# The last two block pairs of a down projection taken together, and their stores on two queues

## The chip, the cores and the metric

The kernel runs on one core of a Trainium2 chip. The metric is the device time of one launch in microseconds. A core has five engines, each with an instruction queue of its own: TensorE (PE, matrix products), VectorE (DVE), ScalarE (ACT), GpSimd (POOL) and SyncE (SP, which only issues transfers). SP, ACT and POOL can each issue DMA transfers; semaphores order the engines among each other. The profile is one execution, recorded by the hardware profiler.

## The reference

Two stages. The first is linear attention with decay over 4 batches, 8 heads, 768 positions and 64 dimensions per head; per block of 64 positions it does this:

```python
intra = np.einsum('bhic,bhjc->bhij', qb, kb) * Dmask[None]
intra = np.einsum('bhij,bhjd->bhid', intra, vb)
inter = np.einsum('bhid,bhde->bhie', qb * lam_pow[None], kv_state)
out[:, :, sl] = intra + inter
kv_state = lam_block * kv_state + np.einsum('bhsd,bhse->bhde', kb * rev_pow, vb)
```

Its output, seen as 3072 tokens of 512 values, goes through a feed-forward block with 2048 inner values:

```python
h = x @ w_in                    # 3072 x 512 by 512 x 2048
g = np.maximum(0.01 * h, h)     # leaky ReLU
return (g @ w_out).astype(np.float32)   # 3072 x 2048 by 2048 x 512
```

q, k, v are float32, the two weights arrive as 64-bit floats and are narrowed on the chip.

## The kernel before, in words

**Tiling.** The tokens are cut into six groups of T = 512 tokens. The inner dimension of 2048 is cut into NP = 8 pairs of two blocks of 128 (`p` = 0 to 7). A float32 product is formed from three TensorE products of float32r parts: each operand is split in parts h, l and m, and h by h, l by l and m by m are added into the same PSUM bank. So one block of 128 by 128 weights by 512 tokens costs three matmuls (`product`, L839 to L842).

**Stages.** Attention makes x; `up` (L704) multiplies by w_in, applies the leaky ReLU and stores g in DRAM; the down projection reads g again. It works on three double groups `pr` of 1024 tokens, each with two groups `gi`. For a group the 512 outputs lie in four PSUM banks, one for each 128 outputs (`c` = 0 to 3): banks X and Z for `gi` = 0, banks Y and V for `gi` = 1 (`BANKS`, L795). Banks 0 and 1 of the last group are Y, banks 2 and 3 are V. Some pairs are combined over both groups by Strassen's scheme (`strassen`), the others go through `plain`: for a pair it loads g of the group (512 KB) into a slot of a ring of five (`unit`), ACT makes the part h, DVE the parts l and m, and PE does 2 blocks x 4 banks x 3 parts = 24 matmuls. The work of the last group ends with the pairs 4, 5, 6 and 7 in `plain`.

**Output.** For the last pair of a group, `plain` is called with `last` and takes the banks one by one: six matmuls finish a bank, then DVE turns it over in 32 by 32 blocks into the staging tile `gst` (`turn_out`, L905), and DMAs store it (`store_out`, L912). A bank's 512 tokens are two halves `m` of 256 tokens, which lie in different places of the output, and a store takes one half and a quarter `a` of the 128 rows: eight stores for four banks, of 128 KB each. In the last group of all (`end`), the banks come in the order 2, 3, 0, 1; banks 2 and 3 are stored for themselves (eight stores of 64 KB), then banks 0 and 1; bank 1, the last, is done in two halves of 256 columns. `ENDS` (L915) names the queue of each of these stores: S for SP, A for ACT, P for POOL.

**Order.** Nothing is scheduled by the language: `Plan` takes all operations with a cost in us, what they read and write, and a rank, and lists them by a greedy simulation. At each step, of all operations on all engines it takes the one that can start first, and the lower rank where two can start together (`emit`, L83). Each engine's queue then has that order. `seq` lists the stages, and an operation's rank is its stage's place there, shifted by its own `rank`; the loads of `unit` come LEAD = 8 stages ahead. The semaphore waits follow from which tile regions overlap. These are put in by the framework.

Of the kernel before, what the change touches and what calls it, by code (L numbers as in the profile page):

```python
# [25 lines left out]
S = 4096.0  # L26
# [10 lines left out]
class Plan:  # L37
# [23 lines left out]
    def add(self, eng, us, fn, reads=(), writes=(), rank=0.0):  # L61

        n, deps = len(self.ops), set()
        for k in reads:
            w, r = self.last.setdefault(k, [None, []])
            if w is not None:
                deps.add(w)
            r.append(n)
        for k in writes:
            w, r = self.last.setdefault(k, [None, []])  # L70
            if w is not None:
                deps.add(w)
            deps.update(r)
            self.last[k] = [n, []]
        deps.discard(n)
        ways = {eng: us} if isinstance(eng, str) else dict(zip(eng, us))
        if self.slack:
            self.more[n] = self.slack
        if self.chain is not None:
            self.chains[self.chain].append(n)  # L80
        self.ops.append((ways, fn, deps, (self.rank + rank, n), set(writes)))
# [81 lines left out]
def kernel(  # L163
# [10 lines left out]
    nc = tc.nc  # L174
    P = 128
# [6 lines left out]
    NP = d_ff // (2 * P)  # L182
    NCH = B * NCB
    GC = 4
    NG = NCH // GC
    T = GC * C
# [12 lines left out]
    NS = 4  # L199
    LEAD = 8.0  # L200
# [4 lines left out]
    C4 = P // 4  # L205
# [32 lines left out]
    HT = T // 2  # L238
# [42 lines left out]
    add = plan.add  # L281
# [75 lines left out]
    def run(c):  # L357

        lo = max(DV, c - c % TURN)
        return lo, c - c % TURN + TURN - lo  # L360
# [423 lines left out]
    acc = {"X": flat[:2], "Z": flat[2:], "Y": [b1[0], b2], "V": [b1[1], bank["pt"]]}  # L784
    ACC = {"X": ["X0", "X1"], "Z": ["Z0", "Z1"], "Y": ["b10", "b2"], "V": ["b11", "pt"]}
# [9 lines left out]
    BANKS = [[("X", 0), ("X", 1), ("Z", 0), ("Z", 1)], [("Y", 0), ("Y", 1), ("V", 0), ("V", 1)]]  # L795
# [72 lines left out]
    def plain(pr, p, gi, lead, last=False, banks=None):  # L868

        g = 2 * pr + gi  # L870
        here = plan.rank
        plan.rank -= lead
        d = G[pr][p].rearrange("p (f h t) -> p f h t", f=2, h=2)[:, :, gi, :]
        j = unit(d, [x for x in plan.last if x[0] == "G" and x[1] in (str(2 * pr), str(2 * pr + 1)) and x[2:4] == f"{p}{gi}"], 2)
        plan.rank = here
        reads = [f"r{z}{j}" for z in "hlm"] + [f"w{z}{p}" for z in "hlm"]

        def go(fs, cs, lo=0, n=T):
            for f in fs:
                for c in cs:  # L880
                    d, i = BANKS[gi][c]
                    product(acc[d][i][:, lo:lo + n], j, f * T + lo,
                            lambda z, f=f, c=c: W[p][z][:, f * 2 * NQ + c * P:f * 2 * NQ + (c + 1) * P], first=pr == p == f == 0, n=n)

        if not last:
            add("PE", 0.227 * 24, lambda: go((0, 1), range(4)), reads, [ACC[d][i] for d, i in BANKS[gi]])
            return
        end = pr == NG // 2 - 1 and gi == 1
        for i, c in enumerate(banks):
            d, b = BANKS[gi][c]  # L890
            parts_ = 2 if end and i == 3 else 1
            for half in range(parts_):
                k = ACC[d][b] + (f"half{half}" if parts_ > 1 else "")
                n = T // parts_
                add("PE", 0.227 * 6 * (1.0 if parts_ == 1 else 0.53), lambda c=c, half=half, n=n: go((0, 1), (c,), half * n, n),
                    reads + ([ACC[d][b]] if parts_ > 1 else []), [k])
                turn_out(c, acc[d][b], [ACC[d][b], k], half * n, n)
                if i == 3 or end and i == 1:
                    cs = sorted(banks[:2] if end and i == 1 else banks[2:] if end else banks)
                    for m in ([half] if parts_ > 1 else range(2)):  # L900
                        store_out(pr, gi, m, cs, end)

    otile = gst.rearrange("p x f (b c j) -> p (x f b) c j", c=4, j=C4)

    def turn_out(c, b, keys, lo, n):  # L905
        nonlocal n_o
        n_o += 1
        o = otile[:, lo // C4:(lo + n) // C4, c, :]
        add("DVE", 0.1 + 0.6 * n / T, lambda: nc.vector.transpose(out=o, in_=b[:, lo:lo + n].rearrange("p (b i) -> p b i", i=C4)), keys,
            [f"o{c}{m}" for m in range(lo // HT, (lo + n) // HT)] + (["gs0", "gs1"] if n_o <= 4 else []), rank=-1.5)  # L910

    def store_out(pr, gi, m, cs, last):  # L912
        t0, n, w = (2 * pr + m) * T + gi * HT, HT // C4, len(cs) * C4

        ENDS = {(8, 0): "PSAP", (8, 1): "PSAP", (4, 0): "SAPP", (4, 1): "SASA"}  # L915
        QUEUES = {"S": ("DMA", 0.5, nc.sync), "A": ("ACT", 0.5, nc.scalar), "P": ("POOL", 0.65, nc.gpsimd)}

        def store(a, q):
            c0 = a * P + cs[0] * C4
            q.dma_start(out=out[t0:t0 + HT, c0:c0 + w].rearrange("(b i) j -> i b j", i=C4),  # L920
                        in_=otile[a * C4:(a + 1) * C4, m * n:(m + 1) * n, cs[0]:cs[-1] + 1, :].rearrange("i b c j -> i b (c j)"))

        for a in range(4):
            e, us, q = QUEUES[ENDS[8 if cs[0] > 1 else 4, m][a] if last else "A"]
            add(e, us, lambda a=a, q=q: store(a, q), [f"o{c}{m}" for c in cs], [], rank=-1.5 if last else 6.0)

    def copy_banks(d, s):
        for i in range(2):
# [2 lines left out]
    def add_banks(d, s):  # L931
        for i in range(2):
            y, key = w32[:, i, :], [f"w32{i}"]
            add("ACT", 0.6, lambda i=i, y=y: nc.scalar.copy(y, acc[s][i]), [ACC[s][i]], key, rank=-LEAD)
            add("DVE", 0.72, lambda i=i, y=y: nc.vector.tensor_tensor(acc[d][i], acc[d][i], y, op=ALU.add), key, [ACC[d][i]], rank=-LEAD)

    seq = [("a", 0), ("a", 1), ("a", 2), ("a", 3), ("wi", 1), ("b", 4), ("r", 4), ("up", 0, 1), ("wi", 0), ("r", 5),
# [26 lines left out]
    for pr in range(NG // 2):  # L964
# [3 lines left out]
        def n(p, gi, r=pr):  # L968
            return ("n", r, p, gi) if p < NP - 1 else ("l", r, p, gi, (0, 1, 2, 3) if gi == 0 else (2, 3, 0, 1))
# [6 lines left out]
        else:  # L976
            i = seq.index(("up", NG - 1, NP - 1))
            seq[i:i] = [n(0, 0)]
            seq += [n(0, 1), n(1, 0), n(1, 1), ("ws", 0), n(2, 0), n(2, 1), ("ws", 1), n(3, 0), n(3, 1), ("ws", 2), n(4, 0), n(5, 0), ("ws", 3), n(6, 0), n(7, 0)]
    seq += [n(p, 1) for p in range(NS, NP)]  # L980

    freed = False
    for n, x in enumerate(seq):
        plan.rank = float(n)
        steady = begin <= n and x[0] in ("r", "up", "wo")
        if x[0] in "abr":
            {"a": alone, "b": begun, "r": round_of}[x[0]](x[1])
        elif x[0] == "ls":
            load_subs(DV)
            turn(DV)  # L990
        elif x[0] == "lt":
            load_subs(sum(run(DV)))
        elif x[0] == "wi":
            w_in(x[1])
        elif x[0] == "up":
            up(*x[1:])
        elif x[0] == "wo":
            w_out(*x[1:])
        elif x[0] == "wp":
            if not freed:  # L1000
                add("DVE", 0.0, lambda: None, [], ["psc", "po", "X0", "X1", "Z0", "Z1"])
                freed = True
            w_out_parts(x[1])
        elif x[0] == "ws":
            if x[1] == 0:
                add("DVE", 0.0, free_attention, [], ATT + [f"e{z}{p}" for z in "hlm" for p in range(NS)])
            w_sums(x[1])
        elif x[0] == "fr":
            add("ACT", 0.0, free_raws, [], [f"raw{i}" for i in range(NRAW)] + ["rh4", "rl4", "rm4", "zr"])
        elif x[0] == "s":  # L1010
            strassen(*x[1:], LEAD)
        elif x[0] == "n":
            plain(*x[1:], LEAD)
        elif x[0] == "copy":
            copy_banks(*x[1:])
        elif x[0] == "add":
            add_banks(*x[1:])
        else:
            plain(*x[1:4], LEAD, True, x[4])
    plan.emit()  # L1020
# [30 lines left out]
```

## Time and profile before

| | us |
|---|---|
| median of 3 runs | 604.32 |
| lowest and highest of them | 602.46, 983.98 |
| the profiled execution's own time | 603.61 |
| its span, first to last instruction | 601.8 |
| PE busy | 587.2 (98%) |
| DVE, ACT, POOL busy | 391.1, 291.7, 135.6 |
| mean granted PE clock | 0.996 |

The span starts with the first instruction of the program. PE's busy time is the union of its matmuls as the profiler models them. The stages of the last double group are seen in the timeline by the tile that a matmul writes: `psc` is X, `po` is Z, `b` is Y and the first bank of V, `pt` the second bank of V. The instructions of the store line are shown as queue entries (SPq, ACTq) where SP or ACT issues, and as POOL where GpSimd does; their duration is that of issuing. When the data has arrived is a time of its own, the landing.

### The profile page before, as it was taken

The page shows a single profiled execution, that of the slowest core. Times are in us where ns is not written, and L with a number is a line of the kernel's source. Part 1 is how long each engine was busy: PE and PEld are TensorE (multiplying, and loading weights), DVE is VectorE, ACT ScalarE, POOL GpSimd, SP SyncE. Part 2 cuts the span into 40 slices and gives each one's busy share as a digit, 9 for nine tenths or more (in the row PEclk, how much of TensorE's full clock was granted, in tenths as well). Part 3 has the DMA queues.
Part 4 walks back from the last instruction along what each step waited for, and adds up shares of the span by engine and source line. Part 5 has one row for each costly group of instructions (what it writes and reads, how often), then busy time and mean ns, then how long its engine had stood idle before and what let it go on. Part 6 is the DMA issues. An engine that isn't in the chain of part 4 may idle for free.

```text
span 601.8 us, 13238 instructions
## 1 busy us (share of the span) xinstructions
PE 587.2 (98%) x5340; PEld 486.4 (81%) x5340; DVE 391.1 (65%) x533; ACT 291.7 (48%) x459; POOL 135.6 (23%) x176
## 2 busy tenths in 40 slices
PE   7899999999999999999999999999999999999995
PEld 6677888888788888888788888888888888888884
DVE  5999772534365664464279749975689595788741
ACT  4678974445555555565587754432244223252300
POOL 1654560554647374230000000000000000000002
PEclk9999999999999999999999999999999999999998
DMA  9998864795889999886688635526467456484433
GB/s 212 231 269 237 238 188 121 180 243 145 223 250 249 257 247 256 256 237 229 201 288 305 213 117 198 159 90 192 125 197 224 168 159 191 121 271 148 161 106 70
DMA packets 161357, 119.89 MB, mean 199 GB/s; under 512 B 98736, under 2 KB 137904, under 8 KB 161296
## 3 DMA queue, kind: packets, MB, share of 16 engines
q1 hardware_dynamic: 146160, 109.40, 62.3%
q10 hardware_dynamic: 12384, 5.58, 3.6%
q0 software_dynamic: 2752, 4.07, 2.7%
q8 instruction: 42, 0.69, 0.5%
q14 instruction: 19, 0.16, 0.1%
HBM read 79.17 MB, written 39.85 MB: 198 GB/s over the span
## 4 chain that ended last, share of the span: by engine, by line
PE 86%; DVE 5%; issue 4%; DMA 2%; SPq 2%; POOL 1%; ACT 1%; POOLq 0%; DVEq 0%; ACTq 0%
PE b L716 40%; PE po L841 12%; PE psc L841 11%; PE b L841 11%; PE pt L841 4%; PE po L328 4%; PE psc L328 3%; SPq L389 1%; DVE w L610 1%; DVE w L609 1%; DMA raws<-in_k_dram 1%; DMA xm<-g 1%; PE pt L418 1%; DMA att<-in_k_dram 1%; DVE att L474 1%
## 5 line engine op out<-in xcount | busy, mean ns | idle before, releaser
L716 PE MATMUL b<-xh,wh 128*128 128x512 f32 (+2 forms) x392 | 103.4, 387 | 1.1 <-ACT xh L522 0.8
L716 PE MATMUL b<-xm,wm 128*128 128x512 f32 (+2 forms) x392 | 104.0, 392 | 0.0
L716 PE MATMUL b<-xl,wl 128*128 128x512 f32 (+2 forms) x392 | 103.2, 387 | 0.6 <-DVE wl L621 0.6
L818 ACT ACTIVATE xh<-xm 128x1024 fp32r<-128x1024 f32 x45 | 47.7, 1061 | 93.4 <-DMA xm<-g 42.6
L716 PEld LDWEIGHTS b<-xh,wh 128*128 128x128 f32 x392 | 72.9, 188 | 16.3 <-ACT xh L522 0.9
L716 PEld LDWEIGHTS b<-xl,wl 128*128 128x128 f32 x392 | 72.8, 188 | 15.7 <-DVE wl L621 1.0
L716 PEld LDWEIGHTS b<-xm,wm 128*128 128x128 f32 x392 | 71.5, 188 | 14.9
L734 ACT ACTIVATE b<-b 128x512 f32<-128x512 f32 (+2 forms) x97 | 56.2, 581 | 55.6 <-PE b L716 55.5
L739 ACT ACTIVATE gs<-b 128x512 f32<-128x512 f32 (+2 forms) x97 | 57.2, 592 | 48.7 <-PE b L716 40.1
L920 POOL DMA_DIRECT2D out_dram<-gs x6 | 3.5, 588 | 319.3 <-issue 319.3
L821 DVE SCALAR_TENSOR_TENSOR xl<-xm,xh 128x1024 fp32r<-128x1024 f32 x45 | 54.8, 1218 | 30.0 <-ACT xh L818 29.2
L825 DVE SCALAR_TENSOR_TENSOR xm<-xl,xh 128x1024 fp32r<-128x1024 f32 x48 | 58.7, 1224 | 3.3
L467 DVE TENSOR_TENSOR att<-psc,att 128x512 f32<-128x512 f32 x24 | 16.5, 687 | 47.1 <-PE psc L328 47.1
L477 POOL TENSOR_TENSOR att<-att 128x256 f32<-128x256 f32 x40 | 33.7, 841 | 38.0 <-DVE att L474 37.9
L438 POOL TENSOR_TENSOR att<-att 128x512 f32<-128x512 f32 (+1 forms) x20 | 24.5, 1223 | 71.4 <-PE po L328 50.0
L389 POOL DMA_DIRECT2D att<-in_q_dram x64 | 39.7, 625 | 3.0 <-DVE att L398 1.7
L609 DVE TENSOR_SCALAR w<-w 128x512 int32<-128x512 int32 x32 | 19.3, 604 | 27.5 <-ACT w L603 27.5
L328 PEld LDWEIGHTS po<-att 64*64 64x64 f32 x1472 | 27.1, 134 | 9.5 <-issue 6.5
L610 DVE CUSTOM_DVE_ANT_0 w<-w,lows 128x1024 uint16<-128x1024 uint16 x32 | 29.8, 930 | 7.5 <-ACT lows L607 6.1
L328 PE MATMUL po<-att 64*64 64x64 f32 x1472 | 32.9, 222 | 1.2 <-DVE att L506 0.5
L841 PE MATMUL b<-xl,wl 128*128 128x512 f32 (+1 forms) x86 | 33.0, 384 | 0.0
L841 PE MATMUL b<-xm,wm 128*128 128x512 f32 (+1 forms) x86 | 33.0, 384 | 0.0
(153 smaller groups left out, 1073.8 us busy)
## 6 DMA issues: line engine op xcount, KB each, us to landing
g<-gs SPq DMA_DIRECT2D x31, 512.0 KB, 3.9
xm<-g SPq DMA_DIRECT2D x25, 512.0 KB, 4.5
xm<-b SPq DMA_DIRECT2D x23, 512.0 KB, 3.8
raws<-in_moe_w_in_dram SPq DMA_DIRECT2D x16, 512.0 KB, 5.4
raws<-in_moe_w_out_dram SPq DMA_DIRECT2D x16, 512.0 KB, 4.5
b<-gs SPq DMA_DIRECT2D x16, 512.0 KB, 4.1
att<-in_k_dram SPq DMA_DIRECT2D x48, 128.0 KB, 4.8
att<-in_v_dram SPq DMA_DIRECT2D x24, 256.0 KB, 5.0
```

Of the source, the lines that this page charges most:

```text
L328: nc.tensor.matmul(dst[HALF[cols]], lhsT=lhsT[HALF[rows]], rhs=rhs[HALF[rows]], start=start, stop=True, skip_group_check=True)
L389: (move if nm == "k" else carry)(0.55 if nm == "k" else QSL, lambda o=o, z=z, e=nc.sync if nm == "k" else nc.gpsimd: e.dma_start(out=o.rea ...
L477: add("POOL", 0.7, lambda new=new, j=j: nc.gpsimd.tensor_tensor(state[(j + 1) % 4], new, _bc(lam_c, 2, D), op=ALU.mult), [f"st{j % 4}", "f ...
L609: add("DVE", 0.42, lambda: nc.vector.tensor_scalar(d, d, 3, None, op0=ALU.logical_shift_left), [], [key])
L610: add("DVE", 1.0, lambda: nc.vector.tensor_tensor(d, d, low, op=ALU.add), [kl], [key])
L716: nc.tensor.matmul(dst, lhsT=w[z][:, kk * 2 * P + f * P:kk * 2 * P + (f + 1) * P], rhs=x[z][:, kk, toks], start=start and kk == 0, stop=kk ...
L734: add("ACT", ns, lambda b=b: nc.scalar.activation(out=b, in_=b, func=AF.Copy, bias=0.0, scale=S + 1.0), [], [kb], rank=-1.5)
L739: add("ACT", t, lambda o=o, x=s_: nc.scalar.activation(out=o, in_=x, func=AF.Prelu, bias=0.0, scale=(1.0 + 1.0 / S) / (WS * U), alpha=0.01 ...
L818: nc.scalar.activation(out=ring[j][0], in_=g(), func=AF.Copy, bias=0.0, scale=NEAR)
L821: nc.vector.scalar_tensor_tensor(ring[j][1], g(), 1.0, ring[j][0].bitcast(F32), op0=ALU.mult, op1=ALU.subtract)
L825: nc.vector.scalar_tensor_tensor(m, l.bitcast(F32), -S, h.bitcast(F32), op0=ALU.mult, op1=ALU.add)
L841: nc.tensor.matmul(dst, lhsT=lhs(z), rhs=ring[j][z][:, col:col + n], start=first and z == 0, stop=z == 2, skip_group_check=True)
```

## The change

The pairs 6 and 7 of the last group are no longer two stages but one (`ending`). It does banks 2 and 3 for pair 6, then banks 2 and 3 for pair 7, each turned over as it is done, and stores both; then banks 0 and 1 for pair 6, and for pair 7 first the half `m` = 0 of bank 0 and of bank 1, then the half `m` = 1 of bank 0 and of bank 1, each half turned over by itself, and the half's four stores follow. All sixteen of these stores are issued by SP and ACT in turns. The outputs of the other groups keep their order and their queue. A bank's half is named in the plan by the bank itself, so the second half waits until the first has been turned over.

```diff
+        def some(c, lo=0, n=T):
+            d, b = BANKS[gi][c]
+            add("PE", 0.227 * 6 * (1.0 if n == T else 0.53), lambda: go((0, 1), (c,), lo, n), reads, [ACC[d][b]])
+
+        if last == "parts":
+            return some
         if not last:
             add("PE", 0.227 * 24, lambda: go((0, 1), range(4)), reads, [ACC[d][i] for d, i in BANKS[gi]])
             return
-        end = pr == NG // 2 - 1 and gi == 1
-        for i, c in enumerate(banks):
-            d, b = BANKS[gi][c]
-            parts_ = 2 if end and i == 3 else 1
-            for half in range(parts_):
-                k = ACC[d][b] + (f"half{half}" if parts_ > 1 else "")
-                n = T // parts_
...
-                turn_out(c, acc[d][b], [ACC[d][b], k], half * n, n)
-                if i == 3 or end and i == 1:
-                    cs = sorted(banks[:2] if end and i == 1 else banks[2:] if end else banks)
-                    for m in ([half] if parts_ > 1 else range(2)):
-                        store_out(pr, gi, m, cs, end)
+        for c in banks:
+            some(c)
+            turn_out(gi, c)
+        for m in range(2):
+            store_out(pr, gi, m, range(4), "AAAA")
+
+    def ending(pr, gi, first, lead):
+
+        one, two = (plain(pr, p, gi, lead, "parts") for p in (first, first + 1))
+        a, z = (2, 3), (0, 1)
+        for x in (one, two):
+            for c in a:
+                x(c)
+                if x is two:
+                    turn_out(gi, c)
+        for m in range(2):
+            store_out(pr, gi, m, a, "SASA")
+        for c in z:
+            one(c)
+        for m in range(2):
+            for c in z:
+                two(c, m * HT, HT)
+                turn_out(gi, c, m * HT, HT)
+            store_out(pr, gi, m, z, "SASA")
...
-        ENDS = {(8, 0): "PSAP", (8, 1): "PSAP", (4, 0): "SAPP", (4, 1): "SASA"}
-        QUEUES = {"S": ("DMA", 0.5, nc.sync), "A": ("ACT", 0.5, nc.scalar), "P": ("POOL", 0.65, nc.gpsimd)}
...
-        for a in range(4):
-            e, us, q = QUEUES[ENDS[8 if cs[0] > 1 else 4, m][a] if last else "A"]
-            add(e, us, lambda a=a, q=q: store(a, q), [f"o{c}{m}" for c in cs], [], rank=-1.5 if last else 6.0)
+        for a, x in enumerate(queues):
+            e, q = {"S": ("DMA", nc.sync), "A": ("ACT", nc.scalar)}[x]
+            add(e, 0.5, lambda a=a, q=q: store(a, q), [f"o{c}{m}" for c in cs], [], rank=6.0 if len(cs) == 4 else -1.5)
...
-    seq += [n(p, 1) for p in range(NS, NP)]
+    seq += [n(p, 1) for p in range(NS, NP - 2)] + [("end", NG // 2 - 1, 1, NP - 2)]
...
+        elif x[0] == "end":
+            ending(*x[1:], LEAD)
```

More of the change, by code (lines that the diff above doesn't have):

```diff
@@ L887, in plain @@
             return
-        end = pr == NG // 2 - 1 and gi == 1
-        for i, c in enumerate(banks):
-            d, b = BANKS[gi][c]
-            parts_ = 2 if end and i == 3 else 1
-            for half in range(parts_):
-                k = ACC[d][b] + (f"half{half}" if parts_ > 1 else "")
-                n = T // parts_
-                add("PE", 0.227 * 6 * (1.0 if parts_ == 1 else 0.53), lambda c=c, half=half, n=n: go((0, 1), (c,), half * n, n),
-                    reads + ([ACC[d][b]] if parts_ > 1 else []), [k])
-                turn_out(c, acc[d][b], [ACC[d][b], k], half * n, n)
-                if i == 3 or end and i == 1:
-                    cs = sorted(banks[:2] if end and i == 1 else banks[2:] if end else banks)
-                    for m in ([half] if parts_ > 1 else range(2)):
-                        store_out(pr, gi, m, cs, end)
+        for c in banks:
+            some(c)
+            turn_out(gi, c)
@@ L903, with turn_out @@
     otile = gst.rearrange("p x f (b c j) -> p (x f b) c j", c=4, j=C4)
-    def turn_out(c, b, keys, lo, n):
+    def turn_out(gi, c, lo=0, n=T):
         nonlocal n_o
         n_o += 1
-        o = otile[:, lo // C4:(lo + n) // C4, c, :]
-        add("DVE", 0.1 + 0.6 * n / T, lambda: nc.vector.transpose(out=o, in_=b[:, lo:lo + n].rearrange("p (b i) -> p b i", i=C4)), keys,
+        d, i = BANKS[gi][c]
+        b, o = acc[d][i], otile[:, lo // C4:(lo + n) // C4, c, :]
+        add("DVE", 0.1 + 0.6 * n / T, lambda: nc.vector.transpose(out=o, in_=b[:, lo:lo + n].rearrange("p (b i) -> p b i", i=C4)), [ACC[d][i]],
@@ L910, in turn_out, with store_out @@
             [f"o{c}{m}" for m in range(lo // HT, (lo + n) // HT)] + (["gs0", "gs1"] if n_o <= 4 else []), rank=-1.5)
-    def store_out(pr, gi, m, cs, last):
+    def store_out(pr, gi, m, cs, queues):
         t0, n, w = (2 * pr + m) * T + gi * HT, HT // C4, len(cs) * C4
-        ENDS = {(8, 0): "PSAP", (8, 1): "PSAP", (4, 0): "SAPP", (4, 1): "SASA"}
-        QUEUES = {"S": ("DMA", 0.5, nc.sync), "A": ("ACT", 0.5, nc.scalar), "P": ("POOL", 0.65, nc.gpsimd)}
         def store(a, q):
```

## The prediction

> **What bounds the kernel now.** I read the page first, for the engine that is busy to the end:
>
> ```profile
> span 601.8 us, 13238 instructions
> ...
> PE   7899999999999999999999999999999999999995
> ...
> PEclk9999999999999999999999999999999999999998
> ```
>
> TensorE (PE) is busy in 39 of 40 slices at a full clock; only the first and the last slice are loose. A slice is 15 us, and the change touches the last 17.5 us alone, so the question is how long PE works there and what follows its last matmul. The timeline of the end, the second view, shows it (columns: start, duration, engine, line, operation):
>
> ```profile
> 589.74 0.39 PE L841 MATMUL b<-xh,wh 128*128 128x512 f32 x1
> ...
> 593.41 4.10 SPq L920 DMA_DIRECT2D out_dram<-gs  x5
> 593.41 4.15 ACTq L920 DMA_DIRECT2D out_dram<-gs  x5
> ...
> 594.01 3.48 POOL L920 DMA_DIRECT2D out_dram<-gs  x6 [319.31 <-issue]
> ...
> 594.41 0.28 PE L841 MATMUL b<-xm,wm 128*128 128x256 f32 x1
> ...
> 595.13 0.28 PE L841 MATMUL b<-xm,wm 128*128 128x256 f32 x1
> 595.45 0.78 DVE L909 STREAM_TRANSPOSE gs<-b 128x256 f32<-128x256 f32 x2 [0.71 <-PE b L841]
> ```
>
> See three things. The last matmul ends at 595.13 + 0.28 = 595.41, and the span at 601.8: 6.4 us come after PE. The first half's last matmul ends at 594.41 + 0.28 = 594.69, and VectorE (DVE) is free from 594.74, yet both half transposes start at 595.45: the first half waits for the second half of its bank. And the last sixteen stores go out on three queues between 593.41 and 597.6. The third view, the store line cut to single queues and moments, gives each store's way to landing; first ACT's second store of the first batch, then ACT's last two:
>
> ```profile
> L920 ACTq DMA_DIRECT2D out_dram<-gs x1: 468/468/468, 593.8 to 593.8; - x1
> ...
> DMA to landing us min/median/max: 2.4/2.4/2.4
> ```
> ```profile
> L920 ACTq DMA_DIRECT2D out_dram<-gs x2: 413/558/703, 596.4 to 596.9; - x2
> ...
> DMA to landing us min/median/max: 3.0/3.4/3.8
> ```
>
> The last store, issued at 596.86, lands 3.8 us later at 600.7; from there to the end it is 1.1 us of closing waits. The windows say why it takes 3.8 and not 2.4 (columns: stretch, length, busy time of PE, weight load, DVE, ACT, POOL, then clock, DMA share, GB/s):
>
> ```profile
> 594.25:596.00 1.75, 1.16 (x10) 0.96 (x8) 1.04 (x3) 0.00 (x0) 1.75 (x4) 1.00 0.97 194
> 596.75:600.25 3.50, 0.00 (x0) 0.00 (x0) 0.00 (x0) 0.00 (x0) 0.74 (x2) 0.62 0.79 172
> ```
>
> From 596.75 to 600.25 the DMA engines carry 172 GB/s x 3.5 us = 0.60 MB, the eight stores issued after 595.9 (64 KB each) and a rest of earlier ones. The end is a queue of stores.
>
> **The change part by part.** Earlier outputs go through the same calls with the same ranks, all on ACT: nothing. Pair 7's operand is asked for one rank earlier; it is ready at 578.2 (the DVE row of L825 at 576.98 lasts 1.23) and needed at 587.0 instead of 589.7. That cover is 8.8 us; were it gone, PE would stall by what is missing, one for one.
>
> *PE order.* Matmuls of 512 columns start 0.227 us apart (593.37, 593.60), so a pair is 24 x 0.227 = 5.44: pair 6 from 584.30, pair 7 from 589.74. The new order does banks 2 and 3 of both pairs first (24 matmuls, the last starts at 589.52 and ends at 589.90), then banks 0 and 1 of pair 6 until 592.46. Then come four halves of six 256-column matmuls, 0.12 apart (594.29, 594.41): 4 x 0.72 = 2.88, where before one whole bank and two halves took 1.36 + 1.44 = 2.80. PE ends 0.08 later.
>
> *Two new waits on PE.* Half 1 of bank 0 must wait for the transpose of half 0 of bank 0, and so for bank 1. Half 0 of bank 0 ends at 593.06 + 0.28 = 593.34; the transpose starts 0.04 later (595.41 to 595.45) and takes 0.45; PE follows 0.05 after a DVE end, as here:
>
> ```profile
> 25.28 0.69 DVE L467 TENSOR_TENSOR att<-psc,att 128x512 f32<-128x512 f32 x1 [1.32 <-PE psc L328]
> ...
> 26.02 0.38 PEld L328 LDWEIGHTS po<-att 64*64 64x64 f32 x20 [0.34 <-DVE att L467]
> ```
>
> That is 593.88, and PE is due there at 593.90, having done bank 1's half meanwhile. The cover is 0.02 us, nearly none. If the wait sits ahead of the weight load, the load is exposed: after a DVE wait at 47.52 the next matmul starts 0.34 later instead of 0.23, so 0.11 a wait. No row shows this wait itself. Bounds: 0, since PE can't start early, to 0.2 for both; I take 0.1, halfway, since both rows are equally near. Behind the waiting matmul stand only the last half banks, and behind these the last stores. PE's last matmul ends at 595.41 + 0.08 + 0.1 = 595.60.
>
> *Transposes.* Before, two halves (0.78) followed PE's end; now only one (0.42) does, the others lie beside PE. It ends at 595.60 + 0.04 + 0.42 = 596.06, against 596.23.
>
> *Stores.* Before: SP 5, ACT 5, POOL 6. After: SP 8, ACT 8. The eight of banks 2 and 3 are issued from 590.69 (bank 3 ends 589.90, transpose 589.94 to 590.66), four on each queue; at 0.3 to 0.5 each (the two rows of 593.41, and eight in a row on ACT at 323/491/501 ns from 575.7) they are out by 592.7. Before, they sat at 593.41 to 596.3. They hide under PE wholly. Half 0's four go out when bank 1's half is turned: 594.06 + 0.1 + 0.04 + 0.42, at 594.62, two to a queue; their queues are then idle. POOL's 3.48 us of issuing lay beside PE and the other queues; taking it off buys nothing by itself, and costs SP and ACT one 0.4 us issue each, beside PE. Half 1's four go out at 596.09 and 596.50, two to a queue. Their price is the term that decides. The nearest row is the batch of 593.41: two stores on each of SP and ACT with little in front, landed at 593.82 + 2.4 = 596.2, which is 2.8 after the batch's first issue. Half 0's stores by the same row have landed by 597.4. So the last store lands at 596.09 + 2.8 = 598.9, against 600.7. Bounds: 2.0 after its own issue (SP's first store of that batch), 598.5; and 3.8, as the last store of before, 600.3.
>
> *Sum.* 598.9 + 1.1 = 600.0 of span, 1.8 less. The profiled execution took 603.61, its span 601.8 and 1.8 around it, so the forecast is 600.0 + 1.8 = **601.8 us**. The median of the runs shown is 604.32, 0.7 above the profiled one; the lowest is 602.46, 1.15 below it. Measured from the median the same saving gives 602.5.
>
> **Rivals.** A: *landing does not shrink*. If the 3.8 is the cost of writing to DRAM just then and not the queue, the last store lands at 596.50 + 3.8 = 600.3, and the time is 603.2. For it: lone-queue stores elsewhere took up to 6.0 to land. Against it: those met 512 KB loads, and at 593.41 the same stores took 2.0 to 2.4.
>
> B: *the last eight are one stream*. The halves' stores, taken together, need the 3.5 us that the last eight needed from 596.75, whichever queue carries them, because half 1's bytes queue behind half 0's. The stream begins 0.8 after 594.62 (595.93 to 596.75 before), ends at 598.9, lands 0.45 later (600.25 to 600.7) at 599.4, and the time is 602.3. For it: with three queues at work the DMA engines are 0.97 busy from 594.25, so a queue more or less adds no rate. Against it: the four stores of 593.41 were through in 2.8 while POOL's were being issued beside them. The Trainium skill, "DMA: Bandwidth & Descriptors", section "Issuing engines are not separate DMA queues", states the rule behind this rival: all queues run on the same 16 DMA engines, and spreading stores over them saves only the time of issuing. By that rule, the trace agrees in the 0.97.
>
> C: *the order is not what the words say*. The planner puts all banks of pair 6 first, because in its own reckoning pair 7's operand is late. Then banks 2 and 3 are ready at 592.6 as now, all sixteen stores (1.05 MB) go from 594.25 at 172 GB/s until 600.4, land 0.45 later, and the time is 603.7. Against it: the 8.8 us of cover.
>
> D, the slower side: *two queues choke on issuing*. Each must issue eight stores in order, and one held up holds all behind. The slowest issue of a store in the trace took 1.63 us. At that, from 590.69, the eighth starts at 590.69 + 7 x 1.63 = 602.1, lands at 604.5, and the time is 607.4. It decides from 1.09 us an issue: then the eighth starts at 598.3 and lands, 2.4 later, at 600.7 as now. For it: issues grow to 0.72 when stores pile up. Against it: eight of twice the bytes went out from one queue at 0.5 each.
>
> **How the numbers follow.** Forecast 0.60, A 0.13, B 0.14, C 0.05, D 0.06, the rest 0.02. Low end: no PE waits, last landing at 598.4, 0.9 of closing: 599.3 of span, 601.1, less the 1.2 by which the lowest run shown lies under the profiled one: 599.9. High end: A with both waits at their upper bound, 603.4, and the 0.7 by which the median lies above: 604.1. B and C lie inside, D outside. A change of 2% is 12 us, about what a measurement of this kernel can tell from no change; no case here reaches it. So within 2% has 0.97; slower 0.02, faster 0.01 are for what I have not seen.
>
> **What would show it.** After: stores of banks 2 and 3 near 590.7; four runs of six 256-column matmuls with gaps under 0.1 between; a single half transpose after PE's end; none of these stores on POOL; the last landing 2.8 to 3.0 after half 1's first issue. A landing 3.8 after its own issue is A if the DMA engines are idle before it, B if they are busy without a break from half 0's stores on; first stores at 593.4 is C; a queue still issuing past 597.5 is D. The prediction is wrong if PE shows gaps before 592, or a stage before 573 has moved.

## The result

The changed kernel took 601.13 us (median of 12 runs, 599.81 to 602.48), the kernel before 603.02 (median of 12, the three of the first table among them). The ratio is 0.9966, with a 95% interval from 0.9956 to 0.9976: 2 us faster, clear of noise, and far within 2%. The run of 983.98 us in the first table stands alone and is left out of the ratio.

The page of the changed kernel, its first rows:

```profile
span 599.5 us, 13248 instructions
...
PE 587.5 (98%) x5346; PEld 487.4 (81%) x5346; DVE 392.5 (65%) x534; ACT 291.5 (49%) x459; POOL 132.8 (22%) x170
```

The span is 2.3 shorter, but not all of that is the change: pair 6's first matmul stood at 584.30 before and stands at 583.83 now, after the same work. The two profiles run their matmuls in the same order up to there and stand 0.47 apart already at 241 us, long before the change. In the eleven profiles of this study pair 6 starts anywhere from 582.81 to 584.72. I therefore measure **the ending**, from pair 6's first matmul to the last instruction: 17.53 us before, 15.69 after, 1.84 less. In a second profile of the changed kernel it was 15.69 again.

The timeline of the ending after (start, duration, engine, line, operation):

```profile
590.21 6.21 SPq L934 DMA_DIRECT2D out_dram<-gs  x8
590.22 6.28 ACTq L934 DMA_DIRECT2D out_dram<-gs  x8
...
591.99 0.28 PE L841 MATMUL b<-xh,wh 128*128 128x256 f32 x1
...
592.90 0.45 DVE L926 STREAM_TRANSPOSE gs<-b 128x256 f32<-128x256 f32 x1 [2.72 <-PE b L841]
...
593.30 0.28 PE L841 MATMUL b<-xm,wm 128*128 128x256 f32 x1
593.40 0.19 PEld L841 LDWEIGHTS b<-xh,wh 128*128 128x128 f32 x1
593.42 0.37 PE L841 MATMUL b<-xh,wh 128*128 128x256 f32 x1
...
593.63 0.28 PE L841 MATMUL b<-xl,wl 128*128 128x256 f32 x1
...
594.22 0.29 PE L841 MATMUL b<-xh,wh 128*128 128x256 f32 x1
594.35 0.28 PE L841 MATMUL b<-xl,wl 128*128 128x256 f32 x1
...
594.82 0.28 PE L841 MATMUL b<-xm,wm 128*128 128x256 f32 x1
595.14 0.45 DVE L926 STREAM_TRANSPOSE gs<-b 128x256 f32<-128x256 f32 x1 [0.27 <-PE b L841]
```

See the first stores at 590.21, the halves from 591.99, and one transpose, not two, after PE's last matmul. At 593.42 the second half of bank 0 begins; the next matmul follows 0.21 later instead of 0.12. That is the first of the two new waits, 0.09 us. Its weight load (PEld) waited too: it starts at 593.40, 0.05 after the transpose's end (592.90 + 0.45) and 0.10 after the matmul before it, where a load otherwise starts with that matmul. At the second, 594.22, the next follows after 0.13: next to nothing. ACT's last two stores, from the store line:

```profile
L934 ACTq DMA_DIRECT2D out_dram<-gs x2: 373/418/462, 595.6 to 596.0; - x2
...
DMA to landing us min/median/max: 2.2/2.2/2.2
```

They land 2.2 after their issue, the last at 598.24, where the last two of before took 3.0 and 3.8.

### The profile page after: what moved, and what is told of

Same layout as the page of the kernel before. It is cut to its first block, busy times and chain, and to the rows that moved or that the text cites. A ratio compares the mean times of both kernels' runs of the same rounds, so it can differ in the third digit from the quotient of the medians.

```text
span 599.5 us, 13248 instructions
## 1 busy us (share of the span) xinstructions
PE 587.5 (98%) x5346; PEld 487.4 (81%) x5346; DVE 392.5 (65%) x534; ACT 291.5 (49%) x459; POOL 132.8 (22%) x170
## 3 DMA queue, kind: packets, MB, share of 16 engines
q0 software_dynamic: 2560, 3.68, 2.5%
## 4 chain that ended last, share of the span: by engine, by line
PE 93%; DVE 5%; DMA 1%; POOL 0%; issue 0%; ACT 0%; DVEq 0%
PE b L716 43%; PE b L841 14%; PE po L841 13%; PE psc L841 11%; PE pt L841 5%; PE po L328 4%; PE psc L328 3%; DVE w L610 1%; DVE w L609 1%; PE pt L418 1%; DMA att<-in_k_dram 1%; DVE att L474 1%; DVE wm L636 1%; DVE wl L621 0%; DVE wh L618 0%; DVE att L467 0%
## 5 line engine op out<-in xcount | busy, mean ns | idle before, releaser
L716 PEld LDWEIGHTS b<-xl,wl 128*128 128x128 f32 x392 | 72.8, 188 | 15.7 <-DVE wl L621 1.0
L438 POOL TENSOR_TENSOR att<-att 128x512 f32<-128x512 f32 (+1 forms) x20 | 24.3, 1215 | 70.9 <-PE po L328 52.5
L841 PE MATMUL b<-xh,wh 128*128 128x512 f32 (+1 forms) x88 | 33.5, 380 | 0.0
L434 POOL TENSOR_TENSOR att<-att 128x512 f32<-128x512 f32 (+1 forms) x23 | 26.9, 1169 | 29.6 <-DMA att<-in_k_dram 10.2
```

The lines of the kernel that those rows point to most:

```text
L434: lambda e="POOL": ENG[e].tensor_tensor(kr[nr], kr[nr], _bc(pow_k, 3, D)[nr], op=ALU.mult), ["fk"], [f"k{i}"])
L716: nc.tensor.matmul(dst, lhsT=w[z][:, kk * 2 * P + f * P:kk * 2 * P + (f + 1) * P], rhs=x[z][:, kk, toks], start=start and kk == 0, stop=kk ...
L841: nc.tensor.matmul(dst, lhsT=lhs(z), rhs=ring[j][z][:, col:col + n], start=first and z == 0, stop=z == 2, skip_group_check=True)
```

## The experiments

All are read by the ending, since its parts are single durations, while the times carry an interval of 0.1%. Each ending comes from one profile; the changed kernel alone was profiled twice. The ratios are to runs of the kernel before that were made beside each. The table gives the moments in us from each span's start; "way" is from the end of the last transpose to the last landing, "closing" from there to the last instruction.

| kernel | pair 6 starts | PE ends | last transpose ends | last landing | ending | way | closing | ratio to before [95%] |
|---|---|---|---|---|---|---|---|---|
| before | 584.30 | 595.41 | 596.23 | 600.68 | 17.53 | 4.45 | 1.15 | |
| changed | 583.83 | 595.10 | 595.59 | 598.24 | 15.69 | 2.65 | 1.28 | 0.9966 [0.9956, 0.9976] |
| e1 queues only | 583.25 | 594.37 | 595.18 | 598.91 | 16.93 | 3.73 | 1.27 | 0.9983 [0.9971, 0.9995] |
| e2 order only | 584.57 | 595.84 | 596.33 | 598.99 | 15.57 | 2.66 | 1.15 | 0.9964 [0.9951, 0.9976] |
| e3 late half | 584.04 | 595.32 | 595.80 | 599.85 | 17.09 | 4.05 | 1.28 | 0.9989 [0.9978, 0.9999] |
| e4 no turns | 584.72 | 595.83 | 596.64 | 600.33 | 16.89 | 3.68 | 1.27 | 0.9993 [0.9982, 1.0003] |
| e5 POOL late | 583.45 | 594.56 | 595.38 | 599.75 | 17.47 | 4.36 | 1.17 | 0.9995 [0.9984, 1.0006] |
| e6 POOL early | 582.81 | 593.92 | 594.74 | 599.08 | 17.30 | 4.34 | 1.03 | 0.9997 [0.9987, 1.0006] |
| e7 covered | 583.03 | 594.32 | 594.81 | 597.57 | 15.90 | 2.76 | 1.37 | 0.9967 [0.9956, 0.9979] |
| e8 changed again | 583.78 | 595.05 | 595.54 | 598.19 | 15.69 | 2.65 | 1.28 | 0.9958 [0.9942, 0.9973] |
| e9 close | 583.41 | 594.68 | 595.17 | 597.84 | 15.57 | 2.67 | 1.15 | 0.9971 [0.9961, 0.9982] |

**e1: the queues alone.** The kernel before, with no store on POOL.

```diff
-        ENDS = {(8, 0): "PSAP", (8, 1): "PSAP", (4, 0): "SAPP", (4, 1): "SASA"}
+        ENDS = {(8, 0): "SASA", (8, 1): "SASA", (4, 0): "SASA", (4, 1): "SASA"}
```

> The kernel before, with its sixteen last stores issued by SP and ACT in turns and none by POOL; the order of the matmuls is as before. I measure the ending: from the first matmul of pair 6 to the last instruction, 17.5 us before (584.30 to 601.8) and 15.7 after (583.83 to 599.5). Theory M (the ending is a backlog: what counts is how many stores are issued at the very end; eight of them need 4.1 us from the first issue to the last landing, four need 2.6): the eight stores of the last two banks still go out together, so most of the time stays; the first eight move from 593.4 on two queues and are out by 595.3, the last one is issued near 597.2 and all 1.05 MB land near 600.2: ending 17.0, ratio to before 0.999. Theory Q (the gain comes from taking the stores off POOL): ending 15.7, ratio 0.997. Theory T (the gain comes from storing the first two banks 3 us earlier): 17.5, ratio 1.000.

Measured 16.93, near the 17.0 of theory M; the eight last stores took 4.03 from first issue to last landing (594.88 to 598.91). Q and T fall as accounts of the whole. But 0.60 for the queues alone is more than the prediction gave them, which was nothing; I come back to this at e5.

**e2: the order alone.** The changed kernel with the queues of before.

```diff
-            store_out(pr, gi, m, a, "SASA")
+            store_out(pr, gi, m, a, "PSAP")
...
-            store_out(pr, gi, m, z, "SASA")
+            store_out(pr, gi, m, z, ("SAPP", "SASA")[m])
...
```

> The changed kernel with its new order of matmuls, transposes and stores, but with the queues as before: POOL issues four of the first eight stores and two of the four of half 0; the last four go out on SP and ACT. M: the last four meet no queue unless POOL's two late stores (issued near 594.1 and 594.7, landed 2.2 to 3.3 later, so by 598) still move beside them: ending 15.7 to 16.0, ratio 0.997. T: the same. Q: 17.5, ratio 1.000.

Measured 15.57, the whole gain and 0.12 more, just under M's 15.7 to 16.0: Q falls for good. POOL's two stores of half 0 were issued at 595.11 and 595.68 and landed by 597.8, and the last four, issued from 596.36, landed 1.9 to 2.2 after their issue, as without POOL. The 0.12 lies in the closing (1.15 against 1.28).

**e3: half 0's stores held back.** Matmuls and transposes as changed; the stores of half 0 stand behind those of half 1.

```diff
-            store_out(pr, gi, m, z, "SASA")
+        store_out(pr, gi, 1, z, "SASA")
+        store_out(pr, gi, 0, z, "SASA", [f"o{c}1" for c in z])
...
```

> The changed kernel, but half 0's four stores stand behind half 1's four in the queues, so all eight go out after the last transpose; matmuls and transposes are untouched. M: eight stores on two queues took 4.09 us from first issue to last landing in the first batch of the changed kernel, four took 2.62, so the end comes 1.5 later: ending 17.1, ratio 0.9993. T (only the early batch counts): 15.7, ratio 0.997. A theory that the last store's way to DRAM costs the same however many go with it gives 0.9 later, from the two further issues of 0.45 on each queue: 16.6, ratio 0.9985.

Measured 17.09: 1.40 of the 1.84 are gone, though PE and DVE work as in the changed kernel. ACT's four, from the store line:

```profile
L935 ACTq DMA_DIRECT2D out_dram<-gs x4: 375/469/480, 595.8 to 597.3; - x4
...
DMA to landing us min/median/max: 2.2/2.5/2.6
```

Two causes add up. The last issue (597.27) comes 1.47 after the last transpose, where it came 0.45 after it in the changed kernel, so 1.0 is issuing; and that store lands 2.6 after its issue, not 2.2, so 0.4 is the queue. The third theory of this expectation, that a store's way costs the same whatever goes with it, counted the issuing alone, gave 16.6 and falls short by 0.5.

**e4: no turns.** Banks 2 and 3 first and stored early, but bank 0 whole and bank 1 in two halves, as before.

```diff
-        for m in range(2):
-            for c in z:
-                two(c, m * HT, HT)
-                turn_out(gi, c, m * HT, HT)
-            store_out(pr, gi, m, z, "SASA")
+        two(0)
+        turn_out(gi, 0)
+        for m in range(2):
+            two(1, m * HT, HT, f"half{m}")
+            turn_out(gi, 1, m * HT, HT, f"half{m}")
+            store_out(pr, gi, m, z, "SASA")
...
```

> The changed kernel with banks 2 and 3 first and stored early, but banks 0 and 1 of pair 7 one after the other as before: bank 0 whole, bank 1 in two halves, and then the stores of half 0 and half 1. Both half transposes then follow PE's end, and eight stores go out after them. M: PE ends 0.17 earlier than in the changed kernel, the first issue comes 0.52 after PE's end, the last landing 4.1 after that: ending 17.0, ratio 0.999; so of the 1.8 us, 0.5 come from the early batch and 1.3 from the turns. T: 15.5 to 15.7, ratio 0.997.

Measured 16.89, near M's 17.0. DVE and ACT in the timeline of e4:

```profile
595.86 0.78 DVE L927 STREAM_TRANSPOSE gs<-b 128x256 f32<-128x256 f32 x2 [0.71 <-PE b L841]
```
```profile
596.35 1.91 ACTq L935 DMA_DIRECT2D out_dram<-gs  x4
```

Both transposes stand behind PE's end (595.83) again, and eight stores behind the first of them. So the early batch by itself is not where the gain is. M's split in my expectation (0.5 from the early batch) was wrong, though: e1 has the same queues without the early batch and ends at 16.93. With no store on POOL, the early batch alone is worth 0.04, the turns 1.20 on top of it (16.89 to 15.69).

**e5 and e6: which of POOL's stores cost the 0.60.** The kernel before, with POOL kept for half 0 alone (e5), or for the first eight alone (e6).

```diff
-        ENDS = {(8, 0): "PSAP", (8, 1): "PSAP", (4, 0): "SAPP", (4, 1): "SASA"}
+        ENDS = {(8, 0): "SASA", (8, 1): "SASA", (4, 0): "SAPP", (4, 1): "SASA"}   # e5
+        ENDS = {(8, 0): "PSAP", (8, 1): "PSAP", (4, 0): "SASA", (4, 1): "SASA"}   # e6
```

> The kernel before, with POOL left out of the first eight stores (SP and ACT issue them) but kept for two of half 0's four. Taking all six stores off POOL shortened the ending of the kernel before from 17.5 to 16.9 us. Theory L (POOL is late: it issues one store in 0.58, so two of its first four and both of half 0's come last, while SP and ACT stand idle): with two stores only, POOL issues them by 596.5 on the clock of before, and most of the gain is there: ending 16.9 to 17.1. Theory S (a store from POOL slows the others beside it: eight stores at the end took 4.75 us with POOL among them and 4.0 without, wherever else POOL is used): ending 17.5, as before.

> The kernel before, with POOL kept for four of the first eight stores and left out of the last eight. L: POOL's four are issued from 594.0 to 596.3 as before and land by 598.6, beside half of the last eight; the last eight, now all on SP and ACT, are issued by 597.3 and land 2.5 later: ending between 17.0 and 17.4. S: the same stretch is shared with POOL's stores until 598.6 only, so a part of the 0.7 goes: 17.2. This run alone can't tell the two apart; with the run that keeps POOL late it says which of POOL's stores cost the 0.6.

Measured 17.47 and 17.30. Counted to the last landing, without the closing, the two stores of e5 bring back 0.64 and the four of e6 0.62 of the 0.72 that e1 had saved there. For e5 theory L gave at most 17.1 and falls; S gave 17.5. For e6 both gave about what was measured. ACT's store of half 1 in e5, issued at 596.18, and ACT's two stores from 596.1 on in e1:

```profile
L920 ACTq DMA_DIRECT2D out_dram<-gs x1: 322/322/322, 596.2 to 596.2; - x1
...
DMA to landing us min/median/max: 3.6/3.6/3.6
```
```profile
L920 ACTq DMA_DIRECT2D out_dram<-gs x2: 323/361/399, 596.1 to 596.5; - x2
...
DMA to landing us min/median/max: 2.4/2.4/2.4
```

With two of POOL's stores beside it, the same store takes 3.6 instead of 2.4. The windows of e5, then of e1, show how the stream ends (stretch, length, PE, weight load, DVE, ACT, POOL, clock, DMA share, GB/s):

```profile
597.90:598.40 0.50, 0.00 (x0) 0.00 (x0) 0.00 (x0) 0.00 (x0) 0.00 (x0) 0.50 1.10 213
598.40:598.90 0.50, 0.00 (x0) 0.00 (x0) 0.00 (x0) 0.00 (x0) 0.00 (x0) 0.50 0.50 100
598.90:599.40 0.50, 0.00 (x0) 0.00 (x0) 0.00 (x0) 0.00 (x0) 0.00 (x0) 0.50 0.17 29
```
```profile
597.20:597.70 0.50, 0.00 (x0) 0.00 (x0) 0.00 (x0) 0.00 (x0) 0.00 (x0) 1.00 1.09 224
597.70:598.20 0.50, 0.00 (x0) 0.00 (x0) 0.00 (x0) 0.00 (x0) 0.00 (x0) 1.00 1.03 213
598.20:598.70 0.50, 0.00 (x0) 0.00 (x0) 0.00 (x0) 0.00 (x0) 0.00 (x0) 1.00 0.52 112
```

In e1 the DMA engines are full until the last half microsecond. In e5 half of their time is idle already from 598.40 and most of it from 598.90, while the last bytes still move. The trace also keeps the sixteen steps in which a store's semaphore counts up, the last of which is the landing. For ACT's last store they lie within 0.33 us in e1; in e5 they spread over 1.18, seven of them by 599.00 and the other nine only from 599.48 on. So a part of the store lags behind the rest. The steps bear no engine's name, and nothing here varies what sets POOL's stores apart (in e5 its two went in 64 packets, the seven of SP and the seven of ACT in 1904 each), so why it lags stays open.

That the batch of eight takes longer with POOL's stores among it or just ahead is shown in three kernels: 4.75 (before), 4.67 (e5) and 4.65 (e6) from first issue to last landing, against 4.03 (e1), 4.02 (e3) and 3.99 (e4) with none. In e6 alone the two theories are not told apart, as the expectation said: POOL's early stores also landed later there (14.4 us after pair 6's start) than SP's and ACT's in e1 (13.3), so more was left to move ahead of the eight.

**e7: three edits on top of the change.** Half 0 of bank 0 before bank 1 of pair 6; POOL for four of the first eight; POOL for one of the last four.

```diff
-            store_out(pr, gi, m, a, "SASA")
-        for c in z:
-            one(c)
+            store_out(pr, gi, m, a, "PSAP")
         for m in range(2):
             for c in z:
+                if m == 0:
+                    one(c)
                 two(c, m * HT, HT)
...
-            store_out(pr, gi, m, z, "SASA")
+            store_out(pr, gi, m, z, ("SASA", "SAPS")[m])
...
```

> The changed kernel with three edits that the traces point to. One: half 0 of bank 0 is done before bank 1 of pair 6, so the transpose that PE waits for lies under six more matmuls; PE's one gap of 0.09 goes. Two: the first eight stores use POOL for four, as before, where they have 3 us to spare; this also moves the place of the last stores in the order of the closing waits, of which seven of 0.06 follow the last landing in the changed kernel. Three: POOL takes one of the last four, so that only SP issues two. By the theory of the backlog: ending 15.7 - 0.1 - 0.2 - 0.25 = 15.1 to 15.4, ratio to before 0.996. If a store from POOL slows those beside it, the last landing comes 2.9 after the last transpose instead of 2.65, and the ending is 15.6.

Measured 15.90, longer than the changed kernel: a miss in every part. PE's gap did not go, it moved to the second half of bank 1:

```profile
593.24 0.28 PE L841 MATMUL b<-xm,wm 128*128 128x256 f32 x1
593.36 0.37 PE L841 MATMUL b<-xh,wh 128*128 128x256 f32 x1
593.57 0.28 PE L841 MATMUL b<-xl,wl 128*128 128x256 f32 x1
```

In the changed kernel the first wait's 0.09 delays all that follows and so covers the second wait; cover the first, and the second is bare: the chain from a half's last matmul to PE's release (0.28 + 0.04 + 0.45 + 0.05 = 0.82) is within 0.02 of what hides it, that matmul's 0.12 and the other half's 0.72. POOL began its store 0.29 after the last transpose where SP and ACT began 0.03 after it, and its landing was the last (597.57). The closing took 1.37; of that 0.1 is POOL's own last wait (DRAIN), which ended at 598.15, after SP's at 598.06.

**e8: the changed kernel again.**

> The changed kernel as it is, once more beside the others. All theories: the ratio on record, 0.9966, within its interval 0.9956 to 0.9976; ending 15.7, the same to 0.1, since the ending's waits don't depend on what the run did before.

Ending 15.69, the same to 0.01; ratio 0.9958 with an interval that overlaps the first.

**e9: the closing.** The changed kernel, with two of the first eight on POOL.

```diff
-            store_out(pr, gi, m, a, "SASA")
+            store_out(pr, gi, m, a, ("PSAP", "SASA")[m])
...
```

> The changed kernel with two of the first eight stores issued by POOL, where they have 3 us to spare; nothing else differs. In the changed kernel the last landing (598.24) is seen by SP's third closing wait, and six more of 0.06 each follow it; the stores of SP and ACT take their semaphores from a ring of eight in turns, so with two stores fewer the last one falls on the semaphore that SP waits for last. Theory: the closing shrinks from 1.28 to 0.9, PE's part (11.27) and the way from the last transpose to the last landing (2.65) stay, ending 15.3 instead of 15.7; ratio to before 0.996, which the times alone can't tell from the changed kernel's 0.9966. Rival (POOL's stores delay whatever follows them): last transpose to last landing 2.8 or more, ending 15.5 to 15.9. Rival (the closing waits run beside the landing in any order): closing 1.28, ending 15.7.

Measured 15.57: closing 1.15, where I expected 0.9, the way 2.67, PE's part 11.27 as it was. SP's closing waits in e9, from the line of the launch:

```profile
L1062 SPq EVENT_SEMAPHORE  x8: 28/28/28, 597.7 to 598.1; - x8
```

Eight waits run from 597.66, when SP's own last store had landed (597.64), and the last landing at 597.84 falls among them. The place of the last store in their order counts, as the theory said; but the next to last landing starts the train, and that sets the floor that I had missed. POOL's two early stores delayed nothing at the end. In their own batch they did: the stores of SP and ACT behind POOL's first landed 3.2 and 3.3 after their issue, the same two in the changed kernel 2.6 and 2.7.

Neither e9 nor e2, with endings 0.12 shorter, can be told from the changed kernel by its time.

## Why the prediction was right, and where it was not

**The sum.** Forecast 1.8 off the ending, measured 1.84. That the two meet so closely is in part luck: the way from the last transpose to the last landing came out 0.19 shorter than the sum had it (2.65 against 2.84), and the closing 0.18 longer. The time itself, 601.13, is below the forecast 601.8 since the kernel before, too, came out lower: 603.02 over 12 runs against the profiled 603.61.

**PE order.** Forecast 0.08 for more halves and 0.1 for the waits; PE's part grew from 11.11 to 11.27, 0.16. The two waits came near the two bounds, 0.11 and 0: the first cost 0.09, the second next to nothing. Up to the first of them PE's matmuls follow one another without a gap, so pair 7's operand was there in time, as forecast.

**Transposes.** From pair 6's start, the last transpose ended 0.17 earlier (11.76 against 11.93); 0.17 was forecast, with PE 0.02 too long and the half transpose 0.03 too short (0.42, measured 0.45). That the first half waits for its bank's second half was right: e4 brings back both transposes behind PE.

**Stores.** The step that carried the forecast. From half 1's first issue to its last landing 2.62 us, against 2.8 in the sum and the 2.8 to 3.0 that was to show it; from the last transpose 2.65 against the 4.45 of before. The row behind the 2.8 had more stores behind its four. In e3 and e4, too, where four follow, the fourth of the last eight landed 2.84 and 2.87 after their first issue, so the term was too long by the 0.2 that the followers add. The closing took 1.28 instead of 1.1 and gave that back; e9 shows that its length depends on which store lands when.

**The step that failed** is the one on POOL: "taking it off buys nothing by itself". In the order of before it buys 0.60 (e1). In the new order it buys nothing and costs 0.12 in the closing (e2), so the sum did not suffer. I had priced POOL by its issuing alone and not by what its stores do to those beside them. So the gain is no plain sum of parts: queues alone 0.60, order alone 1.96, both 1.84.

**Rivals.** A fell: the last store of the changed kernel landed 2.2 after its issue. C fell: the first stores went out at 590.21. D fell: SP and ACT issued in 0.32 to 0.49. B fell, though by little. It needs DMA engines that are busy without a break from half 0's stores on, and the windows of the changed kernel show a break:

```profile
594.95:596.25 1.30, 0.15 (x2) 0.00 (x0) 0.45 (x1) 0.00 (x0) 0.00 (x0) 1.00 0.95 196
596.25:596.45 0.20, 0.00 (x0) 0.00 (x0) 0.00 (x0) 0.00 (x0) 0.00 (x0) 1.00 0.14 30
596.45:597.85 1.40, 0.00 (x0) 0.00 (x0) 0.00 (x0) 0.00 (x0) 0.00 (x0) 1.00 0.90 187
```

Half 0's bytes are through at 596.25 and half 1's begin at 596.45, 0.26 MB each: two batches, not one stream of 3.5 us, and the 2.2 of the last landing shows no queue. But the break is 0.2 us long. Had the halves come closer together, half 1's stores would have queued behind half 0's, as they do in e3, where eight issued together need 4.0.

## What to carry to other kernels

At the end of a kernel count what is issued after the last product, not what is stored in all: eight stores there took 4.0 us and four 2.6, and work that makes the last pieces finish in turns is worth more than moving an earlier batch further ahead. A wait that is covered to within 0.02 us still cost 0.09, and covering it merely bared the next one, so look at the whole cycle of turns. Test a change of queues in the order in which it will run: the same edit was worth 0.60 in one order and cost 0.12 in the other.

## What the runs showed of the hardware that I had not expected

- Stores issued by POOL among eight stores at the end or just ahead of them lengthened the batch from 4.0 to 4.7 us (e5, e6 and the kernel before, against e1, e3 and e4). With POOL's stores ahead of the last four (e2, e9) nothing was lost at the end. The Trainium skill, "DMA: Bandwidth & Descriptors", section "Issuing engines are not separate DMA queues", has it that issuing on several engines at once saves issue time only. Here the measurement differs, and it decides: the third issuing engine cost time.
- After a DVE release that came 0.02 us before PE needed it, the matmul still lost 0.09 us; released 0.10 before, as at 594.22 (its transpose ended at 594.07, and PE follows 0.05 after), it lost 0.01. The weight load ahead of the matmul waited for the same release: it started 0.10 after the matmul before it in the first case and 0.02 after it in the second.
- Each closing wait of SP took 0.06 us one after another. Eight of them in e9 ended half a microsecond after the landing that starts them (597.64 to 598.12), and the last instruction followed 0.86 later; in the changed kernel it followed 0.87 after the last of these waits.
